# Attention with a gated layer behind it: the later head pairs' scores as 64 by 64 products, and one break per pair instead of two

## The chip, the cores and the metric

The kernel runs on one core of a Trainium2 chip. Its time is the device time of one execution in microseconds (us); the lower, the better. The data is float32 in DRAM, and the kernel starts with all inputs there.

## The reference

Causal attention of 4 batches, 12 heads, 448 positions and 64 features per head, and a gated layer of 768 to 1536 to 768 on its output:

```python
scores = (q @ k.transpose(0, 1, 3, 2)) / np.sqrt(64)      # q, k, v: (4, 12, 448, 64)
scores = np.where(np.triu(np.ones((448, 448), bool), k=1), -1e9, scores)
attn = np.exp(scores - scores.max(-1, keepdims=True))
attn = attn / (attn.sum(-1, keepdims=True) + 1e-9)
x = (attn @ v).transpose(0, 2, 1, 3).reshape(1792, 768)
gate = 1 / (1 + np.exp(-(x @ w_gate)))                    # 768 x 1536
return (gate * (x @ w_val)) @ w_out                       # w_out: 1536 x 768
```

## The kernel before

**Work.** The 48 heads are taken as 24 pairs; a pair's two heads lie in partitions 0 to 63 and 64 to 127 of the tile `raw` (448 columns of q, then 448 of k). The layers are computed batch by batch ("units" of 448 tokens): units 0 and 1 by `unit_items`, units 2 and 3 together by `pair_items`, which needs fewer products. Every layer product is split into three fast ones (`xh`,`wh`), (`xl`,`wh`), (`xh`,`wl`) of 128 x 128 by 448 columns; they stand on L610 for units 0 and 1, and on L823 for units 2 and 3. The weights of a product are loaded, and cut into `wh` (ScalarE, L591) and `wl` (VectorE or GpSimd, L593), before it; in unit 0 they come as 64-bit words (L575, 768 KB each), are put together by L579 to L583 and written back to DRAM as float32 (L586), from where the later units read them.

**Attention.** Pairs 0 to 5 are an opening of their own, ahead of the layers. Pairs 6 to 23 are called wide here. For each of them:

- `wscore` makes the scores of four blocks of queries (three of 128, the last of 64) against the keys up to the block's end: two products per block, one for each head, side by side in the two halves of the array's rows. Blocks 0 and 1 go to `s` banks, block 2 to `t` banks, block 3 to `s` banks; in block 3 the two heads' 64 queries take partitions 0 to 63 and 64 to 127.
- `wsoftmax` does the rest of the softmax: a masked minimum on VectorE (L429), exp on ScalarE (L435), sums and reciprocals on VectorE (L443, L445), the scaling on GpSimd (L450).
- `shift` transposes on VectorE (L465, L468) and sends the result through DRAM (`pd` written by L473, four loads of `pt` by L476) to finish the transposition.
- `wpv` multiplies by v (L493): 20 products of 128 rows by 64 columns of the array, each head in one half of the array's columns; its result becomes the layers' input (`features`).

**Order.** Every operation is recorded in a `Plan` with a planned cost and a due time; `Plan.order` then fixes the order on each engine by list scheduling over these, with corrections by hand in `NUDGE` (operation number to shift of the due time). TensorE runs the layers' products without end, and attention's products are put between them in breaks: `together` joins several parts into one operation that isn't cut. Before the change each wide pair n has two breaks: the scores of blocks 0 to 2; and, some 20 products later, `wpv` of pair n-2 with block 3 of pair n. `TURN` and `SPREAD` set over which stretch of the layers' products pairs 6 to 11, and 12 to 23, are spread. When the last pair's `wpv` has been recorded, `pair_inputs` makes the inputs of units 2 and 3. DMAs are issued from one queue (SP) in the planned order: an issue that waits holds up those behind it.

Of the kernel before, what the change touches and what calls it, by code (L numbers as in the profile page):

```python
# [8 lines left out]
F32 = mybir.dt.float32  # L9
# [3 lines left out]
ALU = mybir.AluOpType  # L13
# [33 lines left out]
NUDGE = {  # L47
# [4 lines left out]
}  # L52
# [151 lines left out]
def kernel(  # L204
# [21 lines left out]
    ident = new("ident", [128, 128], F32)  # L226
    mask = new("mask", [128, 4 * WQ], F32)
    pairs = [dict(b=n // HP, k=n % HP) for n in range(B * HP)]
# [166 lines left out]
    rows = lambda i: WQ if i < 3 else WL  # L395
    place = lambda z, i: slice(0, WQ) if i < 3 else slice(WL * z, WL * z + WL)
    keys = lambda i: min(WQ * (i + 1), S)

    def wscore(n, blocks, tag, due):
        j = pairs[n]  # L400
        if blocks[0] == 0:
            j["sm"] = [new("sm", [128, SMW], F32, BUFS["sm"]) for z in range(2)]
            for k in ("mn", "sum", "r"):
                j[k] = new(k, [128, 2, NB], F32, BUFS["st"])
        r = j["raw"]
        sp = [new(tag, [128, 512], F32, dict(s=3, t=2)[tag], PSUM) for z in range(2)]
        base = woff(blocks[0])
# [8 lines left out]
        burst((sum(keys(i) / 600 for i in blocks) + 0.3, mm, [(r,)], [(sp[0],), (sp[1],)]), due)  # L416
        return lambda: wsoftmax(j, blocks, sp)

    def wsoftmax(j, blocks, sp):
        base = woff(blocks[0])  # L420
        mn, su, r_ = j["mn"], j["sum"], j["r"]
        last = blocks[-1] == NB - 1
        for i in blocks:
            ne, off = keys(i), woff(i)
            o = off - base
            for z in range(2):
                y = 0 if last else z
                sm, at, s0 = j["sm"][y], place(z, i), i * WQ - place(z, i).start
                plan.op("DVE", dve(ne), lambda z=z, y=y, sm=sm, i=i, o=o, ne=ne, off=off, s0=s0, at=at: nc.vector.tensor_tensor_reduce(  # L429
                    out=sm.t[at, off:off + ne], in0=sp[z].t[at, o:o + ne], in1=mask.t[at, ZM - s0:ZM - s0 + ne],  # L430
                    scale=-0.125, scalar=3.0e38, op0=ALU.add, op1=ALU.min, accum_out=mn.t[at, y, i:i + 1],
                ), [(sp[z],), (mask,)], [(sm, (i, z)), (mn, (z, i))])
            for z in range(1 if last else 2):
                sm, zs = j["sm"][z], (0, 1) if last else (z,)
                plan.op("ACT", act(ne, 0, 1) + 0.01, lambda z=z, sm=sm, i=i, ne=ne, off=off: nc.scalar.activation(  # L435
                    out=sm.t[:, off:off + ne], in_=sm.t[:, off:off + ne], func=ACTF.Exp, scale=-1.0,
                    bias=mn.t[:, z, i:i + 1], accum_out=su.t[:, z, i:i + 1],
                ), [(mn, *[(y, i) for y in zs])], [(sm, *[(i, y) for y in zs]), (su, (z, i))], extra=0.1)
        g = (0, 0, 1, 2)[blocks[-1]]
        a = slice(blocks[0], blocks[-1] + 1)  # L440
        heads = range(1 if last else 2)
        h = slice(0, len(heads))
        plan.op("DVE", 0.13, lambda: nc.vector.tensor_scalar_add(r_.t[:, h, a], su.t[:, h, a], 1e-9),  # L443
                [(su, *[(z, i) for z in heads for i in blocks])], [(r_, g)])
        plan.op("DVE", 0.11, lambda: nc.vector.reciprocal(r_.t[:, h, a], r_.t[:, h, a]), [], [(r_, g)])  # L445
        for z in heads:
            sm = j["sm"][z]
            for i in blocks:
                o, w = woff(i), keys(i)
                plan.op("PL", 0.24 + w / 1200, lambda sm=sm, i=i, o=o, w=w, z=z: nc.gpsimd.tensor_scalar(  # L450
                    out=sm.t[:, o:o + w], in0=sm.t[:, o:o + w], scalar1=r_.t[:, z, i:i + 1], scalar2=1.0,
                    op0=ALU.mult, op1=ALU.mult), [(r_, g)], [(sm, (i, 0), (i, 1)) if last else (sm, (i, z))])

    def shift(n):
# [7 lines left out]
        for z, i in [(z, i) for i in range(3) for z in range(2)] + [(0, 3)]:  # L462
            sm, o, c, at = j["sm"][z], woff(i), min(i + 1, 3), z * 192 + ioff(i) if i < 3 else 384
            r = [(sm, (i, z))] if i < 3 else [(sm, (i, 0), (i, 1))]
# [36 lines left out]
    def burst(part, due):  # L501
        held.append(part)
# [15 lines left out]
    def att_steps(seq, wide):  # L518

        L = []  # L520
        for m in range(len(seq) + LAG + 1 if seq else 0):
# [5 lines left out]
            if wide:  # L527
                if c is not None:
                    L.append((0, lambda due, c=c: shift(c)))
                one, two = [], []  # L530
                if n is not None:
                    for bl, tag in ((0, 1), "s"), ((2,), "t"):
                        one.append((sum(keys(i) / 600 for i in bl) + 0.2, lambda due, n=n, bl=bl, tag=tag: wscore(n, bl, tag, due)))
                if d is not None:
                    two.append((2.0, lambda due, d=d: wpv(d, due)))
                if n is not None:
                    two.append((0.9, lambda due, n=n: wscore(n, (3,), "s", due)))
                for mine in (one, two):
                    if mine:
                        L.append((sum(w for w, _ in mine), lambda due, mine=mine: together(due, *(f for _, f in mine)), 1.0))  # L540
                    else:
                        L.append((0, lambda due: None, 1.0))
                continue
# [518 lines left out]
def _lay(q, k, v, moe_w_gate, moe_w_val, moe_w_out):  # L1062
# [46 lines left out]
```

## Time and profile before

| what | value |
|---|---|
| median of 3 runs (lowest, highest) | 636.79 us (636.79, 637.36) |
| the profiled execution: its time, its span | 637.35 us, 635.6 us |
| busy: TensorE, VectorE, ScalarE, GpSimd | 627.3, 455.3, 341.6, 316.0 us |
| mean granted clock of TensorE | 0.996 of full speed |
| bytes moved by DMA | 149.74 MB, 236 GB/s |

The span is what the trace covers; 1.75 us of the execution's time lie outside it. Busy time is the union of an engine's instructions, so products that run side by side count once. A float32 product that isn't split by the kernel appears as two records in the trace.

### The profile page before, as it was taken

How to read it: one execution, taken by the hardware profiler on the slowest of the kernel's cores; microseconds unless marked ns; L12 is line 12 of the kernel's file. 1: busy time of each engine (PE TensorE's matmuls, PEld its weight loads, DVE VectorE, ACT ScalarE, POOL GpSimd, SP SyncE). 2: the span in 40 equal slices, each digit the busy share in tenths (PEclk: the TensorE clock that was granted, in tenths of full speed). 3: DMA queues.
4: the chain of work that ended last, by engine and by line, in shares of the span. 5: the costliest groups of instructions: out<-in, count | busy, mean ns of one | idle time of the engine just before them, and what ended most of it. 6: DMA issues, size and time to landing. Idle time of an engine off the chain costs nothing.

```text
span 635.6 us, 10969 instructions
## 1 busy us (share of the span) xinstructions
PE 627.3 (99%) x3750; PEld 534.6 (84%) x3750; DVE 455.3 (72%) x1072; ACT 341.6 (54%) x773; POOL 316.0 (50%) x352
## 2 busy tenths in 40 slices
PE   7999999999999999999999999999999999999997
PEld 4567888888898788788787899999999989999996
DVE  4876999899975765656567965377755568999852
ACT  6877677666645555465555653442433443556520
POOL 4841524535220596676676854764765556700200
PEclk9999999999999999999999999999999999999999
DMA  7467899999998999886787884756423312444311
GB/s 276 147 229 258 308 362 387 331 365 381 308 387 339 325 333 349 303 291 245 254 309 264 289 266 155 270 213 224 156 75 124 102 49 86 134 129 143 114 74 68
DMA packets 50887, 149.74 MB, mean 236 GB/s; under 512 B 5648, under 2 KB 9104, under 8 KB 48528
## 3 DMA queue, kind: packets, MB, share of 16 engines
q1 hardware_dynamic: 50832, 149.05, 66.8%
q8 instruction: 29, 0.48, 0.3%
q14 instruction: 26, 0.21, 0.1%
HBM read 105.78 MB, written 43.25 MB: 234 GB/s over the span
## 4 chain that ended last, share of the span: by engine, by line
PE 95%; ACT 2%; POOL 1%; DVE 1%; DMA 0%; issue 0%; DVEq 0%; ACTq 0%
PE m L610 42%; PE m L823 19%; PE s L823 10%; PE t L823 7%; PE m L493 5%; PE s L414 5%; PE t L414 2%; PE s L292 2%; PE t L343 1%; POOL sm L330 1%; ACT sm L309 1%; PE m L367 1%; ACT pt L352 0%; DMA raw<-in_qkt_dram 0%; PE m L292 0%; ACT wh L591 0%
## 5 line engine op out<-in xcount | busy, mean ns | idle before, releaser
L777 POOL TENSOR_TENSOR wl<-room,wh 128x384 fp32r<-128x384 f32 x84 | 94.7, 1149 | 56.7 <-ACT wh L776 56.7
L610 PE MATMUL m<-xh,wh 128*128 128x448 f32 x288 | 109.2, 379 | 0.0
L610 PE MATMUL m<-xl,wh 128*128 128x448 f32 x288 | 105.2, 365 | 0.0
L610 PE MATMUL m<-xh,wl 128*128 128x448 f32 x288 | 105.2, 365 | 0.0
L450 POOL TENSOR_SCALAR sm<-sm,r 128x384 f32<-128x384 f32 (+3 forms) x126 | 78.9, 642 | 49.8 <-DVE r L445 39.2
L435 ACT ACTIVATE sm<-sm,mn 128x128 f32<-128x128 f32 (+3 forms) x126 | 65.8, 524 | 49.6 <-DVE mn L429 44.4
L593 POOL TENSOR_TENSOR wl<-wr,wh 128x768 fp32r<-128x768 f32 x38 | 72.7, 1916 | 35.8 <-ACT wh L591 35.2
L591 ACT CAST wh<-wr 128x768 fp32r<-128x768 f32 x72 | 59.6, 829 | 33.2 <-PE m L610 12.8
L610 PEld LDWEIGHTS m<-xh,wh 128*128 128x128 f32 x288 | 54.0, 188 | 24.2 <-issue 16.4
L776 ACT CAST wh<-room 128x384 fp32r<-128x384 f32 x84 | 39.7, 511 | 54.8 <-PE s L823 16.8
L610 PEld LDWEIGHTS m<-xh,wl 128*128 128x128 f32 x288 | 54.1, 188 | 4.4
L429 DVE CUSTOM_DVE_ANT_0 sm<-s,mask 128x128 f32<-128x128 f32 (+1 forms) x108 | 44.3, 438 | 18.4 <-PE s L414 17.5
L610 PEld LDWEIGHTS m<-xl,wh 128*128 128x128 f32 x288 | 54.2, 188 | 3.7
L610 PE MATMUL m<-gh,wh 128*128 128x448 f32 x144 | 53.4, 371 | 0.0
L610 PE MATMUL m<-gh,wl 128*128 128x448 f32 x144 | 52.6, 365 | 0.0
L610 PE MATMUL m<-gl,wh 128*128 128x448 f32 x144 | 52.6, 365 | 0.0
L640 POOL TENSOR_TENSOR gl<-gt,gh 128x448 fp32r<-128x448 f32 x24 | 29.8, 1242 | 40.4 <-ACT gh L639 21.5
L465 DVE STREAM_TRANSPOSE room<-sm 128x384 f32<-128x384 f32 (+2 forms) x84 | 34.6, 445 | 18.1 <-POOL sm L450 17.7
L823 PE MATMUL m<-pt,wh 128*128 128x448 f32 x150 | 44.8, 366 | 0.0
L593 DVE TENSOR_TENSOR wl<-wr,wh 128x768 fp32r<-128x768 f32 x34 | 35.1, 1034 | 7.8 <-ACT wh L591 7.6
L692 DVE TENSOR_TENSOR xl<-m,xh 128x448 f32<-128x448 f32 x30 | 18.6, 621 | 28.8 <-PE m L823 28.6
L493 PEld LDWEIGHTS m<-pt,vr 128*64 128x64 f32 x720 | 33.4, 137 | 5.5 <-issue 3.0
(175 smaller groups left out, 1446.9 us busy)
## 6 DMA issues: line engine op xcount, KB each, us to landing
room<-in_wp_dram SPq DMA_DIRECT2D x36, 768.0 KB, 7.7
pt<-pd SPq DMA_DIRECT2D x72, 256.0 KB, 5.1
wr<-wdram SPq DMA_DIRECT2D x45, 384.0 KB, 4.3
room<-wdram SPq DMA_DIRECT2D x45, 384.0 KB, 3.5
wdram<-wr SPq DMA_DIRECT2D x36, 384.0 KB, 7.8
pd<-room SPq DMA_DIRECT2D x12, 1024.0 KB, 5.1
raw<-in_qkt_dram SPq DMA_DIRECT2D x23, 448.0 KB, 5.5
vr<-in_vt_dram SPq DMA_DIRECT2D x24, 256.0 KB, 5.2
```

The source lines that it names most:

```text
L414: nc.tensor.matmul(out=sp[z].t[place(z, i), o:o + ne], lhsT=r.t[h, s0:s0 + rows(i)], rhs=r.t[h, S:S + ne])
L429: plan.op("DVE", dve(ne), lambda z=z, y=y, sm=sm, i=i, o=o, ne=ne, off=off, s0=s0, at=at: nc.vector.tensor_tensor_reduce(out=sm.t[at, off: ...
L435: plan.op("ACT", act(ne, 0, 1) + 0.01, lambda z=z, sm=sm, i=i, ne=ne, off=off: nc.scalar.activation(out=sm.t[:, off:off + ne], in_=sm.t[:, ...
L450: plan.op("PL", 0.24 + w / 1200, lambda sm=sm, i=i, o=o, w=w, z=z: nc.gpsimd.tensor_scalar(out=sm.t[:, o:o + w], in0=sm.t[:, o:o + w], sca ...
L465: plan.op("DVE", dve(128 * c) + 0.03, lambda sm=sm, i=i, o=o, c=c, at=at: nc.vector.transpose(out=tv()[:, :, at:at + 32 * c].rearrange("p ...
L493: nc.tensor.matmul(out=vp.t[64 * z:64 * z + 64, i * WQ:i * WQ + rows(i)], lhsT=v.t[:, c, z], rhs=src, start=(c == 0), stop=(c == i))
L591: plan.op("ACT", act(768), lambda: nc.scalar.copy(hi_.t, t.t), [(t,)], [(hi_,)])
L593: plan.op(eng, cost, lambda: at.tensor_tensor(out=lo_.t, in0=t.t, in1=hi_.t.bitcast(F32), op=ALU.subtract), [(t,), (hi_,)], [(lo_,)], lock ...
L610: nc.tensor.matmul(out=ps.t[:, :S], lhsT=a.t[:, k, :], rhs=b.t if isinstance(b, Buf) else b(), start=(first and z == 0), stop=(last and z ...
L776: plan.op("ACT", act(w), lambda: nc.scalar.copy(f(hi_.t), x()), [(src, at)], [(hi_, e)])
L777: plan.op("PL", 0.97, lambda: nc.gpsimd.tensor_tensor(out=f(lo_.t), in0=x(), in1=f(hi_.t).bitcast(F32), op=ALU.subtract), [(src, at), (hi_ ...
L823: nc.tensor.matmul(out=ps.t[:, :S], lhsT=a.t[:, kw, :], rhs=b.at, start=bool(first and z == 0), stop=bool(last and z == 2), skip_group_che ...
```

## The change

- **Products.** In all four blocks of a wide pair the scores are now products of 64 by 64 of the array (64 rows for a head's features, 64 columns for half of a block's queries): four per block, one for each quarter of the array. Block 3 has only 64 queries per head; there the four quarters are two heads by two halves of the keys (224 each). Two of these four need a head's q and k in the other half of the partitions: `_lay` appends such a copy (64 columns of q, 224 of k) to the input, and `load` brings it by a DMA of its own (128 x 288 words) into the second `sm` tile of the pair, which is not used by block 3 otherwise.
- **Banks.** Blocks 0 and 2 share the pair's two `s` banks, blocks 1 and 3 its two `t` banks; the row half of the array always writes the same bank.
- **Softmax.** Block 3 is two operations of 128 partitions x 224 columns on VectorE, the second starting from the first's minimum (`first`); before, two of 64 x 448. The mask gets 224 more columns for it (three small operations on GpSimd at the start). Sums and reciprocals are done once for blocks 0 to 2 and once for block 3.
- **Breaks.** A wide pair has one break: all its scores, then `wpv` of pair n-2.
- **Due times.** `TURN`, `SPREAD`, the start of pair 6 (0.03 to 0.0) and the table `NUDGE` are new.

```diff
-ZM = 384
+ZM = 3 * QB
+HALF = S // 2
+XW = WL + HALF
-TURN, SPREAD = 0.95, 0.85
+TURN, SPREAD = 0.97, 1.02
 NUDGE = {
-    21: 2.7, 40: -0.7, 42: 1.8, 69: -0.8, 288: 3.1, 289: 3.1, 399: 2.1, 405: 2.1, 414: 2.1, 415: 2.1, 452: 2.1,
...
+    24: 2.3, 43: -2.5, 320: 5.8, 389: 1.5, 401: 2.7, 410: 5.8, 437: -1.9, 451: -1.9, 516: 5.8, 632: 5.8,
...
     def load(n):
...
+        if n >= WIDE:
+            j["sm"] = [new("sm", [128, SMW], F32, BUFS["sm"]) for z in range(2)]
+            x = j["sm"][1]
+            plan.op("SP", dma(128 * XW * 4), lambda: nc.sync.dma_start(
+                out=x.t[:, woff(3):woff(3) + XW], in_=qkt[n][:, 2 * S:]), writes=[(x, "x")], extra=2.8)
...
+        ab = [[new(tag, [128, 512], F32, bufs, PSUM) for z in range(2)] for tag, bufs in (("s", 3), ("t", 2))]
+        sp = [ab[i % 2] for i in range(NB)]
         def mm():
-            for i in blocks:
-                s0, ne, o = i * WQ, keys(i), woff(i) - base
-                for z in range(2):
-                    h = slice(64 * z, 64 * z + 64)
-                    nc.tensor.matmul(out=sp[z].t[place(z, i), o:o + ne], lhsT=r.t[h, s0:s0 + rows(i)], rhs=r.t[h, S:S + ne])
+            for i in range(3):
+                s0, ne, o = i * WQ, keys(i), spot(i)
+                for y in range(2):
+                    for z in range(2):
+                        h, c = slice(64 * z, 64 * z + 64), 64 * (z ^ y)
+                        nc.tensor.matmul(out=sp[i][z].t[c:c + 64, o:o + ne],
+                                         lhsT=r.t[h, s0 + c:s0 + c + 64], rhs=r.t[h, S:S + ne])
+            for y in range(2):
+                for z in range(2):
+                    h, c = slice(64 * z, 64 * z + 64), z ^ y
+                    q, k = (x.t[h, woff(3):woff(3) + WL], x.t[h, woff(3) + WL:woff(3) + XW]) if y else (
+                        r.t[h, 3 * WQ:S], r.t[h, S + HALF * z:S + HALF * (z + 1)])
+                    o = spot(3)
+                    nc.tensor.matmul(out=sp[3][z].t[64 * c:64 * c + 64, o:o + HALF], lhsT=q, rhs=k)
...
-                one, two = [], []
+                mine = []
                 if n is not None:
-                    for bl, tag in ((0, 1), "s"), ((2,), "t"):
-                        one.append((sum(keys(i) / 600 for i in bl) + 0.2, lambda due, n=n, bl=bl, tag=tag: wscore(n, bl, tag, due)))
+                    mine.append((2.0, lambda due, n=n: wscore(n, due)))
                 if d is not None:
-                    two.append((2.0, lambda due, d=d: wpv(d, due)))
-                if n is not None:
-                    two.append((0.9, lambda due, n=n: wscore(n, (3,), "s", due)))
+                    mine.append((2.0, lambda due, d=d: wpv(d, due)))
```

How the program's order changes, at three places (equal rows that follow each other are one row with a count; the last words are the output's shape).

TensorE, one pair in the middle of the kernel, before: its two breaks, `wscore` on L414 and `wpv` on L493, with L610's products between them left out.

```order
L414 MATMUL s<-raw 128x128 x2
L414 MATMUL s<-raw 128x256 x2
L414 MATMUL t<-raw 128x384 x2
...
L493 MATMUL m<-pt,vr 64x128 x12
L493 MATMUL m<-pt,vr 64x64 x8
L414 MATMUL s<-raw 64x448 x2
```

The same on TensorE now, where `wscore` stands on L427 and L435, `wpv` on L515 and the layers' products of units 0 and 1 on L628.

```order
L427 MATMUL s<-raw 64x128 x4
L427 MATMUL t<-raw 64x256 x4
L427 MATMUL s<-raw 64x384 x4
L435 MATMUL t<-raw 64x224 x2
L435 MATMUL t<-sm 64x224 x2
L515 MATMUL m<-pt,vr 64x128 x12
L515 MATMUL m<-pt,vr 64x64 x8
```

Eight products of a pair's scores have become 16, and nothing of L628 stands between them and `wpv` any more. In the middle 36 to 72 products of L628 stand between two breaks; before it were 18 to 24 for most. By the 648 products of unit 0 the scores of 8 wide pairs and `wpv` of 6 are done, before and now, in 17 breaks before and 10 now.

SP, the queue that issues the DMAs, in the middle of the kernel, now (L495 writes a pair's `pd`, L498 loads its `pt`, L279 is the new load, L606 brings weights).

```order
L495 DMA pd<-room 128x2048
L279 DMA sm<-in_qkt_dram 128x288
L606 DMA wr<-wdram_1774 128x768
L606 DMA wr<-wdram_1811 128x768
L285 DMA vr<-in_vt_dram 128x512
L273 DMA raw<-in_qkt_dram 128x896
L498 DMA pt<-pd 128x512 x4
```

The new load of pair n+2 stands right behind the write of pair n's `pd`, as it does in all but the first and last pairs; both wait for pair n's transposes.

TensorE, where units 0 and 1 end and units 2 and 3 begin, now (L841 is the layers' product there, before on L823).

```order
L628 MATMUL m<-gh_4240,wl 128x448
L841 MATMUL t<-xh_4159,wh 128x448
L841 MATMUL t<-xl_4171,wh 128x448
L841 MATMUL t<-xh_4159,wl 128x448
L515 MATMUL m<-pt,vr 64x128 x12
L515 MATMUL m<-pt,vr 64x64 x8
L841 MATMUL t<-xh_4164,wh 128x448
```

The last pair's `wpv` has moved from 108 products ahead of units 2 and 3 to 3 products behind their start. Between the last pair's scores and its `wpv` stand `wpv` of two pairs and 111 products now; before, from its block 3 on, one `wpv` and 90 products.

## Rows read from the trace of the kernel before

**Rows 1.** The page: busy time by engine, then the chain's shares by engine.

```profile
PE 627.3 (99%) x3750; PEld 534.6 (84%) x3750; DVE 455.3 (72%) x1072; ACT 341.6 (54%) x773; POOL 316.0 (50%) x352
...
PE 95%; ACT 2%; POOL 1%; DVE 1%; DMA 0%; issue 0%; DVEq 0%; ACTq 0%
```

**Rows 2.** Waits of TensorE, first and last of four: us in total, times, longest.

```profile
PE s L292 <- DMA raw<-in_qkt_dram: 3.4, 1, 3.4
...
PE s L292 <- DVE mn L305: 0.3, 1, 0.3
```

**Rows 3.** The chain in order of time: start us, us, engine, tile, line, records.

```profile
254.79 0.86 PE s L414 x8
256.29 4.45 PE m L610 x21
260.74 1.93 PE m L493 x40
262.67 0.90 PE s L414 x4
263.56 4.46 PE m L610 x21
...
348.29 5.07 PE m L610 x24
...
355.28 0.90 PE s L414 x4
...
366.81 9.92 PE m L610 x48
376.73 1.93 PE m L493 x40
378.66 22.08 PE m L610 x108
```

**Rows 4.** Timeline of TensorE's weight loads: start, us, operation, shapes, count [idle before].

```profile
247.43 1.86 PEld L493 LDWEIGHTS m<-pt,vr 128*64 128x64 f32 x40 [0.30 <-ACT wh L591]
```

**Rows 5.** Windows: PE, PEld, DVE, ACT, POOL busy us (count); PEclk; DMA share; GB/s.

```profile
70.00:130.00 60.00, 60.00 (x364) 50.62 (x363) 56.90 (x139) 39.68 (x84) 31.44 (x36) 1.00 0.97 353
...
170.00:180.00 10.00, 10.00 (x62) 9.05 (x62) 8.34 (x23) 4.34 (x9) 5.91 (x7) 1.00 0.94 324
180.00:190.00 10.00, 10.00 (x74) 9.29 (x69) 5.95 (x9) 4.82 (x7) 0.00 (x0) 1.00 1.02 419
190.00:200.00 10.00, 10.00 (x54) 9.02 (x54) 4.76 (x6) 3.50 (x5) 0.00 (x0) 1.00 1.03 407
```

**Rows 6.** Timeline of VectorE and TensorE near 207 us: a weight's second half, and its first use.

```profile
206.32 1.16 DVE L593 TENSOR_TENSOR wl<-wr,wh 128x768 fp32r<-128x768 f32 x1 [0.42 <-ACT wh L591]
...
208.18 0.36 PE L610 MATMUL m<-gh,wl 128*128 128x448 f32 x1
```

**Rows 7.** Timeline of the queue SP (the last pair's DMAs); the page's landing time of `pt`.

```profile
362.66 0.32 SPq L473 DMA_DIRECT2D pd<-room  x1
...
368.30 1.74 SPq L476 DMA_DIRECT2D pt<-pd  x4
...
pt<-pd SPq DMA_DIRECT2D x72, 256.0 KB, 5.1
```

**Rows 8.** Timeline of TensorE before the first wide pair; the page's landing time of `raw`.

```profile
50.38 0.74 PE L343 MATMUL t<-ident,sm 112*112 112x112 f32 x4
...
58.38 0.93 PE L414 MATMUL s<-raw 64*128 64x128 f32 x8
...
raw<-in_qkt_dram SPq DMA_DIRECT2D x23, 448.0 KB, 5.5
```

**Rows 9.** Timeline of VectorE in block 3, and of GpSimd near the start.

```profile
208.33 0.60 DVE L429 CUSTOM_DVE_ANT_0 sm<-s,mask 64x448 f32<-64x448 f32 x1
208.87 0.07 DVE L429 DVE_READ_ACCUMULATOR2_ANT mn<- 64x1 f32 x1
...
10.57 1.92 POOL L330 TENSOR_SCALAR sm<-sm,r 112x112 f32<-112x112 f32 x4 [8.12 <-ACT sm L309]
```

More of the change, by code (lines that the diff above doesn't have):

```diff
@@ L226 @@
     ident = new("ident", [128, 128], F32)
-    mask = new("mask", [128, 4 * WQ], F32)
+    mask = new("mask", [128, ZM + WQ + HALF], F32)
     pairs = [dict(b=n // HP, k=n % HP) for n in range(B * HP)]
@@ L249, in keep @@
             plan.op("PL", 0.6, lambda: nc.gpsimd.affine_select(
-                out=t.t, in_=t.t, pattern=[[-1, n]], compare_op=cmp, fill=v, base=base, channel_multiplier=1
+                out=t.t[:, :n], in_=t.t[:, :n], pattern=[[-1, n]], compare_op=cmp, fill=v, base=base, channel_multiplier=1
             ), writes=[(t,)])
         fill(mask, 0.0)
-        keep(mask, 4 * WQ, ALU.is_ge, -8.0e9, ZM)
+        keep(mask, ZM + WQ, ALU.is_ge, -8.0e9, ZM)
         fill(ident, 1.0)
         keep(ident, 128, ALU.is_equal, 0.0, 0)
+        end = lambda: mask.t[:, ZM + WQ + HALF - WL:]
+        for step, base, v in (-1, -WL, -8.0e9), (0, -WL, 0.0), (-1, 0, -8.0e9):
+            plan.op("PL", 0.3, lambda step=step, base=base, v=v: nc.gpsimd.affine_select(
+                out=end(), in_=end(), pattern=[[step, WL]], compare_op=ALU.is_ge, fill=v, base=base, channel_multiplier=1
+            ), [(mask,)], [(mask, "end")])
     def load(n):
@@ L395, with wscore @@
     rows = lambda i: WQ if i < 3 else WL
-    place = lambda z, i: slice(0, WQ) if i < 3 else slice(WL * z, WL * z + WL)
     keys = lambda i: min(WQ * (i + 1), S)
-    def wscore(n, blocks, tag, due):
+    spot = lambda i: (384, 0, 0, 256)[i]
+    def wscore(n, due):
         j = pairs[n]
[L401 to L407, printed above, removed]
-        def mm():
+        for k in ("mn", "sum", "r"):
+            j[k] = new(k, [128, 2, NB], F32, BUFS["st"])
+        r, x = j["raw"], j["sm"][1]
+        ab = [[new(tag, [128, 512], F32, bufs, PSUM) for z in range(2)] for tag, bufs in (("s", 3), ("t", 2))]
+        sp = [ab[i % 2] for i in range(NB)]
+        def mm():
+            for i in range(3):
[12 more added lines that the diff above has]
+                    nc.tensor.matmul(out=sp[3][z].t[64 * c:64 * c + 64, o:o + HALF], lhsT=q, rhs=k)
+        burst((1.95, mm, [(r, 0, 1), (x, "x")], [(p,) for p in ab[0] + ab[1]]), due)
+        return lambda: wsoftmax(j, sp)
@@ L410, in mm, with wsoftmax @@
+    def wsoftmax(j, sp):
+        mn, su, r_ = j["mn"], j["sum"], j["r"]
+        for blocks in (0, 1, 2), (3,):
+            last = blocks[0] == 3
+            heads = range(1 if last else 2)
             for i in blocks:
-                s0, ne, o = i * WQ, keys(i), woff(i) - base
+                ne, off, o = keys(i), woff(i), spot(i)
                 for z in range(2):
-                    h = slice(64 * z, 64 * z + 64)
-                    nc.tensor.matmul(out=sp[z].t[place(z, i), o:o + ne], lhsT=r.t[h, s0:s0 + rows(i)], rhs=r.t[h, S:S + ne])
@@ L416, in wscore @@
[L416 to L422, printed above, removed]
-        for i in blocks:
-            ne, off = keys(i), woff(i)
-            o = off - base
-            for z in range(2):
[L427 to L452, printed above, removed]
@@ new lines, in wsoftmax @@
+                    sm, n = j["sm"][0 if last else z], HALF if last else ne
+                    f, lo = (off + HALF * z, (ZM + WQ) * z) if last else (off, ZM - i * WQ)
+                    to = 1 - z if last else z
+                    first = lambda z=z, i=i, last=last: mn.t[:, 1, i:i + 1] if last and z else 3.0e38
+                    plan.op("DVE", dve(n), lambda z=z, i=i, sm=sm, n=n, o=o, f=f, lo=lo, to=to, first=first: nc.vector.tensor_tensor_reduce(
+                        out=sm.t[:, f:f + n], in0=sp[i][z].t[:, o:o + n], in1=mask.t[:, lo:lo + n], scale=-0.125, scalar=first(),
+                        op0=ALU.add, op1=ALU.min, accum_out=mn.t[:, to, i:i + 1],
+                    ), [(sp[i][z],), (mask, "end") if last and z else (mask,)] + ([(mn, (1, i))] if last and z else []),
+                        [(sm, (i, z) if last else i), (mn, (to, i))])
@@ new lines, in wsoftmax @@
+                for z in heads:
+                    sm = j["sm"][z]
+                    plan.op("ACT", act(ne, 0, 1) + 0.01, lambda z=z, sm=sm, i=i, ne=ne, off=off: nc.scalar.activation(
+                        out=sm.t[:, off:off + ne], in_=sm.t[:, off:off + ne], func=ACTF.Exp, scale=-1.0,
+                        bias=mn.t[:, z, i:i + 1], accum_out=su.t[:, z, i:i + 1],
+                    ), [(mn, (z, i))], [*([(sm, (i, 0), (i, 1))] if last else []), (sm, i), (su, (z, i))], extra=0.1)
+            a = slice(blocks[0], blocks[-1] + 1)
@@ new lines, in wsoftmax @@
+            h = slice(0, len(heads))
+            plan.op("DVE", 0.13, lambda h=h, a=a: nc.vector.tensor_scalar_add(r_.t[:, h, a], su.t[:, h, a], 1e-9),
+                    [(su, *[(z, i) for z in heads for i in blocks])], [(r_, last)])
+            plan.op("DVE", 0.11, lambda h=h, a=a: nc.vector.reciprocal(r_.t[:, h, a], r_.t[:, h, a]), [], [(r_, last)])
+            for z in heads:
+                sm = j["sm"][z]
+                for i in blocks:
+                    o, w = woff(i), keys(i)
+                    plan.op("PL", 0.24 + w / 1200, lambda sm=sm, i=i, o=o, w=w, z=z: nc.gpsimd.tensor_scalar(
+                        out=sm.t[:, o:o + w], in0=sm.t[:, o:o + w], scalar1=r_.t[:, z, i:i + 1], scalar2=1.0,
+                        op0=ALU.mult, op1=ALU.mult), [(r_, last)], [(sm, i)])
@@ L463, in shift @@
             sm, o, c, at = j["sm"][z], woff(i), min(i + 1, 3), z * 192 + ioff(i) if i < 3 else 384
[L464 removed]
+            r = [(sm, i)]
             plan.op("DVE", dve(128 * c) + 0.03, lambda sm=sm, i=i, o=o, c=c, at=at: nc.vector.transpose(
@@ L470, in shift @@
             in_=sm.t[:, woff(3) + 384:woff(3) + 448].rearrange("p (r j) -> p r j", j=32)),
-            [(j["sm"][0], (3, 0), (3, 1))], [(tb, "end")])
+            [(j["sm"][0], 3)], [(tb, "end")])
         pd = new("pd", [128, 4 * WC], F32, 2, bass.MemoryType.DRAM)
@@ L529, in att_steps @@
                     L.append((0, lambda due, c=c: shift(c)))
-                one, two = [], []
+                mine = []
                 if n is not None:
-                    for bl, tag in ((0, 1), "s"), ((2,), "t"):
-                        one.append((sum(keys(i) / 600 for i in bl) + 0.2, lambda due, n=n, bl=bl, tag=tag: wscore(n, bl, tag, due)))
+                    mine.append((2.0, lambda due, n=n: wscore(n, due)))
                 if d is not None:
-                    two.append((2.0, lambda due, d=d: wpv(d, due)))
-                if n is not None:
-                    two.append((0.9, lambda due, n=n: wscore(n, (3,), "s", due)))
[L538 to L542, printed above, removed]
+                    mine.append((2.0, lambda due, d=d: wpv(d, due)))
+                if mine:
+                    L.append((sum(w for w, _ in mine), lambda due, mine=mine: together(due, *(f for _, f in mine)), 1.0))
+                else:
+                    L.append((0, lambda due: None, 1.0))
                 continue
@@ L1027 @@
     att = []
-    for seq, wide, lo, hi in ((range(HP, WIDE), False, 0.0, 0.03), (range(WIDE, 2 * HP), True, 0.03, TURN), (last, True, TURN, 1 + SPREAD)):
+    for seq, wide, lo, hi in ((range(HP, WIDE), False, 0.0, 0.03), (range(WIDE, 2 * HP), True, 0.0, TURN), (last, True, TURN, 1 + SPREAD)):
         steps = att_steps(seq, wide)
@@ L1067, in _lay @@
     qkt[0] = np.concatenate([x[:, :2 * QB], x[:, S:], x[:, 2 * QB:S]], axis=1)
+    qkt = np.concatenate([qkt, np.zeros((B * HP, 128, XW), qkt.dtype)], axis=2)
+    x = qkt[WIDE:]
+    for z, (lo, hi) in enumerate(((0, HALF), (HALF, S))):
+        a, b = slice(64 * z, 64 * z + 64), slice(64 - 64 * z, 128 - 64 * z)
+        x[:, a, 2 * S:2 * S + WL] = x[:, b, 3 * WQ:S]
+        x[:, a, 2 * S + WL:] = x[:, b, S + lo:S + hi]
     vt = np.zeros((B * HP, 128, NB, 2, D), v.dtype)
```

7 rows, old and new, of the table NUDGE are left out of this document.

## The prediction, made before the changed kernel ran

> **What bounds the kernel now.** I read the page first, then TensorE's waits, the chain in order of time, and the windows. TensorE is busy for 627.3 us of the 635.6 us span and makes up 95% of the chain [rows 1]. It waits for another engine or a DMA four times in all, 3.4 us for the first load and 0.3 to 0.6 us for the rest, all in the opening [rows 2]. From 57 us on, the chain is TensorE's own work in its own order [rows 3]. So each us that leaves TensorE's stream leaves the time, as long as what it consumes (weights, `pt`) comes earlier by as much.
>
> The price of a break is read from the chain's pieces [rows 3]. 108 products of L610 take 22.08 us and 48 take 9.92 us: (22.08 - 9.92) / 60 = 0.203 us for a product, and 9.92 - 48 x 0.203 = 0.19 us left over for a run between two breaks, whatever its length (21 products: 4.45 - 4.26 = 0.19). A break thus costs 0.19 us beside its own work. One wide pair in the steady part:
>
> - blocks 0 to 2, from 254.79 to 256.29: 1.50 us
> - `wpv`: 1.93 us
> - block 3, from 262.67 to 263.56: 0.90 us
> - two breaks: 0.38 us, together 4.71 us.
>
> **The change, part by part.** *Block 3.* Two products of 448 columns, side by side on two of the array's four quarters, become four of 224 columns on all four. If four quarters run at once, the columns that pass halve, and so does the time: 0.90 to 0.45 us. Rows 3 show each pairing but never four at once. Block 3 gives 0.90 / 448 = 2.0 ns per column of a product. Blocks 0 to 2 have 6 products with 1536 columns, 3.1 us at that price one after the other; they take 1.50 us, so the two row halves run side by side. `wpv` has 20 products with 2048 columns, 4.1 us one after the other; it takes 1.93, so the two column halves do too, though both use all the rows.
>
> *Blocks 0 to 2.* Twelve products of 64 by 64 replace six of 64 by 128. With four at once, the columns that pass are the same 768: 1.50 us again. Bounds: not below, since no column goes. Above: with two at a time, twice as much, 3.0 us (a rival, below). In between: if a block's second pair of products starts only as the first pair's second record does, the last record of block 3 stands alone, 0.22 us (half of its new 0.45 us). The number of instructions is not the limit by `wpv`, which puts 40 records and 40 weight loads through in 1.93 us, 48 ns each; the new scores have 32 in 1.95 us. I take 1.50.
>
> A rule of the Trainium skill speaks against this. What the trace shows: in `wpv` the two column halves use the same rows, and its 40 weight loads keep the loader busy for 1.86 us [rows 4] of the 1.93 us [rows 3] in which products run on without a wait. The Trainium skill, TensorE: Matmul & The Clock Gate, section Part 3: Packing small matmuls, says that a weight load overlaps a running matmul only if the two use different row groups. By that rule the two quarters of one row half would take turns, and the sum would be the first rival's 660 us; `wpv` by the same rule would take some 4.1 us, and the trace does not agree.
>
> *Breaks.* 18 score breaks and 20 others (18 with block 3, two with `wpv` alone) become 20. Sum of TensorE over the 18 wide pairs: before 18 x (1.50 + 1.93 + 0.90) + 38 x 0.19 = 85.2 us; now 18 x (1.50 + 1.93 + 0.45) + 20 x 0.19 = 73.6 us. Gain 11.5 us; 7.5 us with the lone 0.22 us for each pair.
>
> *VectorE, GpSimd, DMA.* Block 3 on VectorE falls from two operations of 0.54 us (208.33 to 208.87) [rows 9] to two of half the columns, some 0.5 us less a pair, and one pair of small sums and reciprocals goes. That is off the chain, but it helps at 70 to 130 us, where VectorE is busy for 56.9 us of 60 [rows 5]. The three mask operations fall into GpSimd's idle 8.12 us before 10.57 us [rows 9]: nothing. The new load is 147 KB a pair. For the first wide pair it can start when the transposes of pair 4 end (51.1 us) and, by the landing time of the larger `raw`, 5.5 us, is there at 56.6 us, ahead of the scores at 58.4 us [rows 8]: nothing, but with 2 us to spare.
>
> **What is late next.** Two covers get thin.
>
> First, the weights of unit 0. From 180 to 200 us the DMA engines are full (share 1.02 and 1.03 at 419 and 407 GB/s) [rows 5], and at the end of that a weight's second half is ready at 207.48 us and used at 208.18 [rows 6]: 0.7 us of slack. By the end of unit 0, 8 pairs have saved 0.45 us each and 7 breaks are gone: TensorE comes 8 x 0.45 + 7 x 0.19 = 4.9 us earlier. If the transfers don't come earlier too, 4.9 - 0.7 = 4.2 us are given back there, for good. The eight new loads by then (1.2 MB, 2.9 us at 407 GB/s) work in the same direction. Against it: at 170 to 180 us the DMA moved 324 GB/s, so there is room ahead of the full stretch. Between 0 and 4.2 us I take 2.5 us.
>
> Second, `pt`. The last pair's six first blocks end at 348.29 us and its block 3 at 356.18 [rows 3]; its `pd` is issued at 362.66, the last of its `pt` by 370.04, and lands some 4.7 us later (5.1 us from issue), near 374.7 [rows 7]; `wpv` starts at 376.73. From the end of block 3 to landing it is 18.5 us, from the end of the six blocks 26.4 us. Now all scores end together, and `wpv` follows two breaks later: in the middle, with 42 and 48 products between, 1.93 + (42 x 0.203 + 0.19) + 3.88 + (48 x 0.203 + 0.19) + 1.95 = 26.4 us; for the last pair 2 x 1.93 + 111 x 0.203 + 3 x 0.19 = 27.0 us. So the spare time is between 0 and 8 us. I take 0.5 us for all pairs together; 1 us a pair would be 12 us. Behind a waiting `wpv` nothing on TensorE can pass.
>
> Sum: 637.35 - 11.5 + 2.5 + 0.5 = 628.85 us for an execution like the profiled one, which is 0.56 us above the median of 636.79: 628.3 us.
>
> **The rivals.**
>
> *Quarters take turns* (slower). If only two of four run at once, a pair's scores cost 1.50 + 0.45 = 1.95 us more than I count, 35 us over 18 pairs: 636.8 - 11.5 + 35.1 = 660 us. It decides from 0.64 us more a pair (11.5 / 18). For it: no row has four at once. Against it: both pairings run freely [rows 3, 4], and the four need nothing that these two don't.
>
> *The gain waits* (no change, or slightly slower). Full DMA engines give back 4.2 us, `pt` comes 0.3 to 0.7 us late for each of the last 12 pairs (4 to 8 us), or the last `wpv`, now 3 products into units 2 and 3, holds those up: 633 to 638 us. For it: 0.7 us of slack and the lower end of `pt`'s spare time. Against it: TensorE never waits after the opening now, and VectorE has less to do.
>
> *Four at once, but not freely* (a smaller gain): the lone 0.22 us for each pair and full give-back, 7.5 - 4.2 - 0.5 = 2.8 us: 634 us; without give-back 629 us.
>
> *Nothing is given back* (counted as the low end of the forecast): 636.8 - 11.5 = 625 us.
>
> **How the numbers follow.** My forecast with 0 to 4.2 us of give-back (624 to 630 us, the low end with 1 us for what the new due times may do to the opening) 0.60; four not freely (629 to 634) 0.13; the gain waits 0.14; quarters take turns 0.13. The time of the likeliest is 628.3 us. The range reaches from 624 to 637.5 us and leaves out the turns, most of all. No change is within 0.2% (1.3 us, about what a measurement tells from none): a third of "the gain waits", 0.05; slower is the turns and a sixth of it, 0.15; the rest, 0.80, is faster.
>
> **What would show it.** Right: in the chain the pieces of L427 and L435 together take 1.9 to 2.0 us, L515 1.93 us, with one leftover of 0.19 us; four records of a block start within some ns of each other; TensorE's waits after 57 us are few, near 200 to 230 us, for `wl` or the weights' DMA. Wrong: pieces of L427 of 3 us (turns); waits of L515 for `pt` pair after pair; a wait of L841 for the weights or inputs of units 2 and 3 right behind the last L515; or an opening that ends later than 58 us.

## The result, and the profile after

The changed kernel takes 625.67 us (median of 4 runs, 625.09 to 627.05) against 636.83 us for the kernel before in the same measurement (636.79 to 637.36): a ratio of 0.9826, 95% interval 0.9808 to 0.9844. That is 11.2 us less. Forecast were 628.3 us, 8.5 us less, in a range from 624 to 637.5 us. The profiled execution took 625.28 us, its span is 623.6 us (before 637.35 and 635.6).

Busy time by engine, and the chain's shares by engine, from the page of the changed kernel; they answer to [rows 1].

```profile
PE 612.9 (98%) x4038; PEld 532.6 (85%) x4038; DVE 448.9 (72%) x1036; ACT 339.0 (54%) x773; POOL 310.9 (50%) x355
...
PE 87%; ACT 4%; DVE 3%; DMA 2%; POOL 2%; issue 2%; SPq 0%; DVEq 0%; POOLq 0%; ACTq 0%
```

TensorE is busy for 14.4 us less, though it has 288 records more. It is still nearly always busy, but its share of the chain fell from 95% to 87%: for some stretches something else now ends last.

The chain in order of time of the changed kernel, one pair in the middle; it answers to [rows 3].

```profile
243.73 0.38 PE s L427 x8
244.11 0.43 PE t L427 x8
244.54 0.64 PE s L427 x8
245.19 0.38 PE t L435 x8
245.56 1.93 PE m L515 x40
247.49 9.92 PE m L628 x48
```

All scores of a pair take 0.38 + 0.43 + 0.64 + 0.38 = 1.83 us, from 243.73 to 245.56, where before blocks 0 to 2 took 1.50 and block 3 0.90, together 2.40. `wpv` takes the same 1.93 us. The run of 48 products takes the same 9.92 us as before, so 0.19 us are left over for a break, as before.

The timeline of TensorE in one pair's scores, changed kernel.

```profile
231.19 0.45 PE L427 MATMUL s<-raw 64*64 64x128 f32 x8
231.46 0.61 PE L427 MATMUL t<-raw 64*64 64x256 f32 x8
231.89 0.82 PE L427 MATMUL s<-raw 64*64 64x384 f32 x8
232.54 0.36 PE L435 MATMUL t<-raw 64*64 64x224 f32 x2
232.55 0.36 PE L435 MATMUL t<-sm 64*64 64x224 f32 x2
232.73 0.36 PE L435 MATMUL t<-raw 64*64 64x224 f32 x2
232.74 0.35 PE L435 MATMUL t<-sm 64*64 64x224 f32 x2
233.02 2.00 PE L515 MATMUL m<-pt,vr 128*64 128x128 f32 x40
```

Here the four quarters are seen at once: block 3's first four records (two from `raw`, two from the copy in `sm`) start at 232.54 and 232.55, their second four 0.19 us later.

TensorE's waits after the opening, from the list of waits of the changed kernel (us in total, times, longest); before there were none.

```profile
PE m L628 <- DVE wl L611: 0.3, 1, 0.3
...
PE m L841 <- DVE xl L710: 0.3, 1, 0.3
```

The timeline of TensorE and VectorE at the first of these; it answers to [rows 6].

```profile
183.87 0.36 PE L628 MATMUL m<-gl,wh 128*128 128x448 f32 x1
184.55 0.47 PE L628 MATMUL m<-gh,wl 128*128 128x448 f32 x1 [0.32 <-DVE wl L611]
...
183.54 0.96 DVE L611 TENSOR_TENSOR wl<-wr,wh 128x768 fp32r<-128x768 f32 x1 [0.96 <-ACT wh L609]
```

From 183.87 to 184.55 it is 0.68 us between two products instead of 0.20: 0.48 us lost for a weight that is ready at 184.50. Another 0.27 us are lost at 219.38, and 0.25 us more than before near 521 us. Together that is 1.0 us of give-back; with the wider steps next to these three (0.28 to 0.31 us instead of 0.20) it is 1.4 us.

Windows of the changed kernel; they answer to [rows 5].

```profile
160.00:170.00 10.00, 10.00 (x51) 9.27 (x50) 8.38 (x17) 5.70 (x10) 6.19 (x9) 1.00 1.01 384
170.00:180.00 10.00, 10.00 (x80) 9.09 (x79) 7.52 (x12) 5.17 (x7) 0.00 (x0) 1.00 0.98 356
180.00:190.00 10.00, 9.68 (x46) 8.31 (x46) 5.36 (x7) 3.71 (x5) 0.00 (x0) 1.00 1.02 405
```

The DMA engines are full from 160 us on now, where before 170 to 180 us ran at 0.94 and 324 GB/s: the transfers have moved ahead with TensorE.

The whole account, from the starts of TensorE's records between the first wide pair's scores and the end: scores 43.2 us before, 33.0 us now, 10.2 less; `wpv` 34.65 and 34.66 us; products of units 0 and 1 with their breaks and waits 264.4 and 261.9 us, 2.5 less, of which 0.6 are three products that now run earlier, in the opening; units 2 and 3 0.3 us more to the start of their last product.

The 1.9 us that remain in units 0 and 1 are a difference. These products stand in 39 runs before and 21 now; at 0.19 us each, 18 runs fewer are 3.4 us less. So some 1.5 us are given back there: 1.15 us at the two waits near 184 and 219 us, and 0.6 us in two runs (81 products from 92.47 us, 72 from 343.20) that start a product every 0.207 us instead of every 0.203, with no wait in the list; the kernel before loses 0.2 us in such runs. What slows them is not shown.

The two profiled executions differ by 12.1 us, the medians by 11.2. The one of the kernel before has a stretch at the lower clock in its opening:

```profile
12.99:16.40 3.41, 3.41 (x20) 2.49 (x18) 2.05 (x6) 2.59 (x6) 2.94 (x6) 0.50 0.39 143
```

Its first wide pair starts at 58.38 us; in before_pv_less_early (below), the same program up to there without such a stretch, it starts at 57.79. So some 0.6 us of the 12.1 are no gain. The changed kernel starts its first wide pair at 58.52 us with three products of L628 (0.6 us) more done: the opening itself takes about as long as before.

### The profile page after: what moved, and what is told of

It reads as the page before. It is cut to its first block, busy times and chain, and to the rows that moved or that the text cites. A ratio compares the mean times of both kernels' runs of the same rounds, so it can differ in the third digit from the quotient of the medians.

```text
span 623.6 us, 11552 instructions
## 1 busy us (share of the span) xinstructions
PE 612.9 (98%) x4038; PEld 532.6 (85%) x4038; DVE 448.9 (72%) x1036; ACT 339.0 (54%) x773; POOL 310.9 (50%) x355
## 4 chain that ended last, share of the span: by engine, by line
PE 87%; ACT 4%; DVE 3%; DMA 2%; POOL 2%; issue 2%; SPq 0%; DVEq 0%; POOLq 0%; ACTq 0%
PE m L628 37%; PE m L841 19%; PE s L841 10%; PE t L841 7%; PE m L515 5%; PE s L427 3%; ACT sm L323 2%; DMA wdram<-wr 1%; PE t L427 1%; PE s L306 1%; PE t L435 1%; PE t L357 1%; POOL sm L472 1%; PE m L381 1%; POOL sm L344 1%
## 5 line engine op out<-in xcount | busy, mean ns | idle before, releaser
L795 POOL TENSOR_TENSOR wl<-room,wh 128x384 fp32r<-128x384 f32 x84 | 98.8, 1199 | 56.5 <-ACT wh L794 52.3
L628 PE MATMUL m<-xh,wh 128*128 128x448 f32 x288 | 107.5, 373 | 0.0
L472 POOL TENSOR_SCALAR sm<-sm,r 128x256 f32<-128x256 f32 (+3 forms) x126 | 70.3, 578 | 74.0 <-DVE r L467 40.4
L628 PE MATMUL m<-xh,wl 128*128 128x448 f32 x288 | 105.4, 366 | 0.1
L628 PE MATMUL m<-xl,wh 128*128 128x448 f32 x288 | 105.3, 365 | 0.0
L611 POOL TENSOR_TENSOR wl<-wr,wh 128x768 fp32r<-128x768 f32 x38 | 69.9, 1857 | 18.7 <-ACT wh L609 18.5
L459 ACT ACTIVATE sm<-sm,mn 128x256 f32<-128x256 f32 (+3 forms) x126 | 65.5, 523 | 7.3 <-DVE mn L452 7.3
L628 PEld LDWEIGHTS m<-xh,wh 128*128 128x128 f32 x288 | 54.1, 188 | 7.0 <-issue 1.8
L628 PEld LDWEIGHTS m<-xh,wl 128*128 128x128 f32 x288 | 54.1, 188 | 4.8 <-POOL wl L611 0.5
L628 PEld LDWEIGHTS m<-xl,wh 128*128 128x128 f32 x288 | 54.2, 188 | 4.0
L628 PE MATMUL m<-gh,wh 128*128 128x448 f32 x144 | 53.6, 372 | 0.0
L628 PE MATMUL m<-gh,wl 128*128 128x448 f32 x144 | 52.8, 367 | 0.3 <-DVE wl L611 0.3
L628 PE MATMUL m<-gl,wh 128*128 128x448 f32 x144 | 52.7, 366 | 0.0
L841 PE MATMUL m<-pt,wh 128*128 128x448 f32 x150 | 44.8, 367 | 0.3 <-DVE xl L710 0.3
L452 DVE CUSTOM_DVE_ANT_0 sm<-s,mask 128x128 f32<-128x128 f32 (+1 forms) x72 | 29.3, 417 | 19.7 <-PE s L427 19.7
L611 DVE TENSOR_TENSOR wl<-wr,wh 128x768 fp32r<-128x768 f32 x34 | 34.7, 1019 | 11.2 <-ACT wh L609 10.9
L515 PEld LDWEIGHTS m<-pt,vr 128*64 128x64 f32 x720 | 33.4, 137 | 5.9 <-issue 4.9
L601 DVE SCALAR_TENSOR_TENSOR wr<-room,wr 128x768 int32<-128x768 int32 x36 | 36.7, 1020 | 0.5
```

Source lines behind the costliest of these rows:

```text
L515: nc.tensor.matmul(out=vp.t[64 * z:64 * z + 64, i * WQ:i * WQ + rows(i)], lhsT=v.t[:, c, z], rhs=src, start=(c == 0), stop=(c == i))
L601: plan.op("DVE", 0.87, lambda: nc.vector.scalar_tensor_tensor(out=ri(), in0=lo(), scalar=29, in1=ri(), op0=ALU.logical_shift_right, op1=AL ...
L611: plan.op(eng, cost, lambda: at.tensor_tensor(out=lo_.t, in0=t.t, in1=hi_.t.bitcast(F32), op=ALU.subtract), [(t,), (hi_,)], [(lo_,)], lock ...
L628: nc.tensor.matmul(out=ps.t[:, :S], lhsT=a.t[:, k, :], rhs=b.t if isinstance(b, Buf) else b(), start=(first and z == 0), stop=(last and z ...
L795: plan.op("PL", 0.97, lambda: nc.gpsimd.tensor_tensor(out=f(lo_.t), in0=x(), in1=f(hi_.t).bitcast(F32), op=ALU.subtract), [(src, at), (hi_ ...
L841: nc.tensor.matmul(out=ps.t[:, :S], lhsT=a.t[:, kw, :], rhs=b.at, start=bool(first and z == 0), stop=bool(last and z == 2), skip_group_che ...
```

## The experiments

My theory: the gain is TensorE's own time, first from the four quarters in block 3, then from fewer breaks; a little is given back in waits. The rivals: the merged break and the new due times bring it, whatever form the products have; or the gain was larger and went back through the new load or the supply of weights.

**block3_alone: the four quarters of block 3 put into the kernel before.** Everything else of the products is as before (two breaks, the old due times, 64 by 128 in blocks 0 to 2); the new load and the longer mask come with it. The planned cost of block 3 is lower too, and the order is another one between 178 and 221 us.

```diff
     def mm():
+        if blocks[0] == 3:
+            for y in range(2):
+                for z in range(2):
...
+                    nc.tensor.matmul(out=sp[z].t[64 * c:64 * c + 64, :HALF], lhsT=q, rhs=k)
+            return
         for i in blocks:
```

Expected:

> The kernel before, with block 3 alone in four quarters (its two breaks, its due times and its 64 by 128 products in blocks 0 to 2 kept; the new load and the longer mask added). If four quarters at once are where the gain comes from, block 3's piece falls from 0.90 to about 0.48 us: 18 x 0.42 = 7.6 us less, 629 us (627.5 to 631). If the gain came from the merged break and the new due times, about 637 us, as before. If the extra load in the same queue costs something in unit 0, up to 3 us above 629.

Measured: 631.98 us (631.76 to 632.05), ratio to before 0.9920 (0.9907 to 0.9934): 4.8 us less, not 7.6. The chain in order of time of this kernel:

```profile
251.95 0.86 PE s L437 x8
252.81 0.65 PE t L437 x4
253.45 4.45 PE m L640 x21
257.90 1.93 PE m L523 x40
259.83 0.54 PE s L431 x8
```

Block 3 fell from 0.90 to 0.54 us, 18 x 0.36 = 6.5 us. Some 1.4 us of that are lost between 204 and 221 us, where the order has shifted: 0.5 us in steps that end with a weight (at 204.49 and 209.22), and 0.87 us at one pair, whose blocks 0 to 2 now follow block 3 of the pair ahead at once and wait until VectorE has read scores (L452):

```profile
218.59 0.49 PE L437 MATMUL s<-raw 64*128 64x128 f32 x2
219.47 0.70 PE L437 MATMUL s<-raw 64*128 64x128 f32 x5 [0.40 <-DVE mn L452]
```

The rival that it is the breaks and due times alone falls: with no break merged and no due time changed, over two fifths of the gain are there. My number missed by 0.06 us a pair, 1.1 us in all, and by the 1.4 us of these waits, which I had not counted.

**wide_rows: blocks 0 to 2 as 64 by 128 again,** in the changed kernel; only block 3 is in quarters.

```diff
-                for y in range(2):
-                    for z in range(2):
-                        h, c = slice(64 * z, 64 * z + 64), 64 * (z ^ y)
-                        nc.tensor.matmul(out=sp[i][z].t[c:c + 64, o:o + ne],
-                                         lhsT=r.t[h, s0 + c:s0 + c + 64], rhs=r.t[h, S:S + ne])
+                for z in range(2):
+                    h = slice(64 * z, 64 * z + 64)
+                    nc.tensor.matmul(out=sp[i][z].t[:, o:o + ne], lhsT=r.t[h, s0:s0 + WQ], rhs=r.t[h, S:S + ne])
```

Expected:

> The changed kernel, with blocks 0 to 2 as six products of 64 by 128 again, block 3 in quarters, one break. If only the columns that pass count, 625.7 us, within 0.6. If a change between the two ways of dividing the array costs what one costs elsewhere (0.1 to 0.15 us between wpv and block 3 before), and the first weights of 128 columns cost 0.05 us more, 18 x 0.15 to 0.20 = 2.7 to 3.6 us more: 628.8 us. If 64 by 64 products had been costly in themselves, less than 625 us.

Measured: 629.59 us (629.40 to 630.32), ratio to before 0.9885 (0.9872 to 0.9899), 3.9 us above the changed kernel. The timeline of TensorE in one pair's scores:

```profile
246.19 0.49 PE L426 MATMUL s<-raw 64*128 64x128 f32 x4
246.51 0.60 PE L426 MATMUL t<-raw 64*128 64x256 f32 x4
246.95 0.81 PE L426 MATMUL s<-raw 64*128 64x384 f32 x4
247.69 0.41 PE L433 MATMUL t<-raw 64*64 64x224 f32 x2
...
248.23 0.98 PE L513 MATMUL m<-pt,vr 128*64 128x128 f32 x14
```

From 246.19 to 248.23 it is 2.04 us, 0.21 more than the 1.83 of the changed kernel, and 18 x 0.21 = 3.8 us. Against the timeline above, start to start: block 0 takes 0.32 us instead of 0.27; block 1, 0.44 and 0.43; block 2, at whose end the array changes its division, 0.74 instead of 0.65; block 3, 0.54 instead of 0.48. So the form 64 by 64 saves nothing in columns, as counted, but it keeps all scores in one division of the array. Block 3 takes 0.54 us wherever it follows another division, here and in block3_alone.

The Trainium skill, TensorEngine Tiling (Array Packing), section Key Properties, says that changing the tiling mode, not just the tile, drains TensorE. The trace agrees as far as it goes: block 1, with no change of division at either end, differs by 0.01 us, and block 2, with one at its end, by 0.09 us. The page gives no figure for it.

**two_breaks: `wpv` in a break of its own,** a few products behind the scores, in the changed kernel.

```diff
+APART = 2.5
...
+    def apart(due, *steps):
...
+        for e, p in enumerate(parts):
+            plan.op("PE", p[0], p[1], p[2], p[3], due + APART * e, count=e == 0)
...
-                    L.append((sum(w for w, _ in mine), lambda due, mine=mine: together(due, *(f for _, f in mine)), 1.0))
+                    L.append((sum(w for w, _ in mine), lambda due, mine=mine: apart(due, *(f for _, f in mine)), 1.0))
```

(`count` keeps the added operations out of the numbers that `NUDGE` uses.) Expected:

> The changed kernel, with wpv put behind up to 12 more of the layers' products, in a break of its own, in 15 of the 16 pairs where it stood behind the scores. If a break costs by itself (0.15 to 0.19 us), 2.3 to 2.9 us more than the changed kernel: 628.3 us. If the merging is not where time went, 625.7 us, within 0.5.

Measured: 629.07 us (628.06 to 630.90), ratio to before 0.9878 (0.9861 to 0.9895), 3.4 us above the changed kernel. From the list of waits of this kernel, then its chain in order of time at one pair's `wpv`:

```profile
PE m L520 <- DMA vr<-in_vt_dram: 1.1, 1, 1.1
...
PE m L520 <- ACT gt L664: 0.9, 1, 0.9
...
PE m L520 <- DMA pt<-pd: 0.2, 1, 0.2
```

```profile
261.08 0.80 PE m L643 x3
261.89 1.93 PE m L520 x40
263.81 9.32 PE m L643 x45
```

The trace has 14 pairs whose `wpv` follows scores at once in the changed kernel, not 16, and 13 of them are apart here: 35 breaks instead of 22, of which one was in units 2 and 3. A run of three products takes 0.80 us, 0.19 more than three times 0.203, and one of 45 leaves 0.19 over too: the price of a break is 0.19 us, as read before the change, even for a run this short. The products of units 0 and 1 with their breaks and waits take 4.2 us more in the profiled execution (266.1 us for 261.9), of which 14 breaks are 2.7 us. The rest is waits: 2.2 us of `wpv` are new, and 0.8 us that the changed kernel lost near 184 us are gone. These come from the other order.

**no_copy: without the new load.** Block 3's second pair of products takes q and k of the wrong head from `raw`, so the output isn't the reference's.

```diff
-            plan.op("SP", dma(128 * XW * 4), lambda: nc.sync.dma_start(
-                out=x.t[:, woff(3):woff(3) + XW], in_=qkt[n][:, 2 * S:]), writes=[(x, "x")], extra=2.8)
...
-                    q, k = (x.t[h, woff(3):woff(3) + WL], x.t[h, woff(3) + WL:woff(3) + XW]) if y else (
-                        r.t[h, 3 * WQ:S], r.t[h, S + HALF * z:S + HALF * (z + 1)])
+                    q, k = r.t[h, 3 * WQ:S], r.t[h, S + HALF * z:S + HALF * (z + 1)]
```

Expected:

> The changed kernel without the new load: block 3's second pair of products takes q and k of the wrong head from raw, so its result isn't the reference's. If the load is hidden, at most the two waits for weights near 184 and 219 us (0.75 us in all) go: 625 to 625.7 us. If the full DMA engines of unit 0 pay for the loads, 2 to 3 us less: 623 us.

Measured: 625.64 us (625.14 to 625.97), ratio to before 0.9823 (0.9810 to 0.9837): the changed kernel's time. In its profiled execution the two waits near 184 and 219 us are gone, and a wait of 0.3 us of `wpv` for its `vr` near 190 us is there instead. So the new load costs nothing that stands out from the spread of these runs.

**pv_less_early and before_pv_less_early: how much room the supply of TensorE has in unit 0.** For pairs 6 to 11, `wpv` does 8 of its 20 products (each block of queries takes its own 128 keys alone, so the output isn't the reference's), in the changed kernel and in the kernel before. The planned order is the same.

```diff
-                for c in range(i + 1):
+                for c in range(i if b < PAIR else 0, i + 1):
...
-                                         start=(c == 0), stop=(c == i))
+                                         start=(c == (i if b < PAIR else 0)), stop=(c == i))
```

Expected of the first:

> The changed kernel with 8 of the 20 products of wpv for pairs 6 to 11 (each block of queries takes its own 128 keys alone, so the result isn't the reference's); the planned order is unchanged. wpv falls from 1.93 to some 0.9 us. If TensorE still sets the time at 90 to 190 us, 6 x 1.05 = 6.3 us less than the changed kernel: 619.4 us. If the supply of unit 0's weights sets it now (slack of 0.5 us from 163 us on), nearly nothing less: 624 to 625.7 us.

and of the second:

> The kernel before with the same 12 products of wpv left out for pairs 6 to 11. If the supply of weights had room of about 5 us there, the room that the change has used, nearly all of 6.3 us: 630.5 to 632 us. If it had none but the 0.7 us of slack near 208 us, 635.5 to 636.5 us.

Measured: 622.78 us (622.67 to 623.02), 2.9 us less than the changed kernel; and 631.94 us (631.69 to 632.76), 4.9 us less than the kernel before (ratios to before 0.9779, 0.9764 to 0.9793, and 0.9924, 0.9909 to 0.9939). In both, `wpv` takes 6.0 us less on TensorE (34.65 to 28.62 us). So the kernel before kept 4.9 of 6.0 us, and the changed kernel 2.9 of 6.0. Windows of pv_less_early, then its two longest waits behind the opening:

```profile
160.00:170.00 10.00, 8.63 (x55) 7.61 (x54) 9.10 (x19) 4.34 (x8) 5.79 (x9) 1.00 1.00 375
...
180.00:190.00 10.00, 9.39 (x56) 7.69 (x55) 5.57 (x8) 4.67 (x7) 0.00 (x0) 1.00 1.04 415
```

```profile
PE m L515 <- DMA vr<-in_vt_dram: 1.4, 1, 1.4
...
PE s L427 <- DMA raw<-in_qkt_dram: 0.6, 1, 0.6
```

TensorE is idle for 1.37 us in the first of these windows and 0.61 us in the second, with the DMA engines full. The first is the wait for a pair's v, the second two waits for weights: what runs short is what the DMAs bring as a whole, weights and a pair's own loads, and not the weights alone. Both of my cases were too plain: TensorE could come 4.9 us earlier before the change, and can come 2.9 us earlier still after it, though its 648th product of L628 starts at 210.26 us now against 216.55 before (L610), 0.6 of which is the lower clock in the opening.

**pv_less_late: the same for pairs 12 to 23,** in the changed kernel (`b >= PAIR` in the lines above; again not the reference's output). Expected:

> The changed kernel with the same 12 products of wpv left out for pairs 12 to 23 instead. If TensorE sets the time in units 1 to 3, 12 x 1.05 = 12.6 us less than the changed kernel: 613 us. If pt or the weights are about to take over there, waits of L515 or L628 give back a part: 616 us or more.

Measured: 618.78 us (617.59 to 619.88), ratio to before 0.9715 (0.9700 to 0.9730): 6.9 us less than the changed kernel of the 12.1 us that `wpv` saves (34.66 to 22.59 us). Waits of this kernel, then TensorE's timeline at the longest:

```profile
PE m L628 <- POOL wl L611: 1.8, 1, 1.8
```

```profile
346.44 0.37 PE L628 MATMUL m<-gl,wh 128*128 128x448 f32 x1
348.64 0.48 PE L628 MATMUL m<-gh,wl 128*128 128x448 f32 x1 [1.84 <-POOL wl L611]
```

Here GpSimd sets the time: it cuts the weights (L611) and scales the scores (L472), and a weight comes 2.0 us late. The stretch at the lower clock behind it (last section) costs 1.5 us more, so 3.5 of the 5.2 us that don't arrive are lost at this one place. So TensorE is the bound in unit 1 only by a narrow margin too. Units 2 and 3 begin 6.0 us earlier (380.15 us for 386.14) and take as long as in the changed kernel, 235.5 us without the last `wpv`: there nothing is given back.

**no_nudge: the changed kernel with an empty `NUDGE`.**

```diff
-NUDGE = {
-    24: 2.3, 43: -2.5, 320: 5.8, 389: 1.5, 401: 2.7, 410: 5.8, 437: -1.9, 451: -1.9, 516: 5.8, 632: 5.8,
...
-}
+NUDGE = {}
```

Expected:

> The changed kernel with an empty table NUDGE. If the new table carries part of the gain by taking waits away, several us more than the changed kernel (628 to 634 us), with waits of TensorE in the trace that show where. If it doesn't matter, 625.7 us, within 1.

Measured: 629.31 us (628.51 to 630.43), ratio to before 0.9886 (0.9870 to 0.9903), 3.6 us above the changed kernel. From its list of waits:

```profile
PE m L622 <- DVE wl L605: 1.1, 3, 0.5
...
PE m L622 <- ACT wh L603: 0.3, 1, 0.3
```

Between 160 and 200 us its products lose 3.1 us in steps of 0.4 to 0.7 us, all for weights, where the changed kernel loses 0.9 us in the same runs of products. So two thirds of the gain need no table, and the table's part is to keep the weights ahead of TensorE in unit 0. The kernel before has a table of its own; what it would take without one no run shows.

## Why the prediction was right

The mechanism was right but for one cost that it left out, that of a change between two divisions of the array. Four sizes were off, and that the time came within 2.6 us of the forecast is partly luck, since the misses have both signs.

- **Block 3 in four quarters: 0.45 us less a pair forecast.** In kind as forecast: all four quarters run at once, and the rival in which they take turns (660 us) is out, by the starts at 232.54 and 232.55. Taken by itself it is 0.36 us (block3_alone), 1.6 us less over 18 pairs than forecast. Block 3 takes 0.54 us behind another division and 0.48 us behind its own, so the change of division is a part that doesn't halve.
- **Blocks 0 to 2 at no change: mis-sized, the largest miss.** I counted columns, which stayed. The form 64 by 64 saves 0.21 us a pair by keeping one division through all scores (wide_rows, 3.9 us in all). Together 0.57 us a pair instead of 0.45, 1.83 us where 1.9 to 2.0 were forecast: 10.2 us of scores instead of 8.1.
- **Breaks: 18 fewer, 3.4 us forecast.** The price of 0.19 us holds, by the runs of 48 products in the changed kernel and of 3 in two_breaks. The count was off: the traces have 39 breaks before, not 38, as `wpv` stands alone three times and not two, and 22 now, not 20, as it stands alone four times. The 17 fewer are 3.2 us.
- **Give-back: 3.0 us forecast, some 1.7 us measured** (1.5 us in units 0 and 1, and 0.2 us near 521 us). I took 2.5 of at most 4.2 us for unit 0's weights, as 0.7 us was the smallest slack near 208 us and the DMA engines were full from 180 to 200 us. The slack near 208 us was that of one weight in an order that the change rearranges; before_pv_less_early shows that the supply of the kernel before could follow a TensorE that is 6 us faster for all but 1.1 us. Part of the room was where I had named it and not counted it: at 170 to 180 us the DMA engines still had some.
- **Together** 10.2 + 3.2 - 1.7 = 11.7 us less, against 11.2 us between the medians.
- **`pt`: 0.5 us forecast.** No wait of L515 is in the trace of the changed kernel. For its last pair the scores end at 360.2 us, the last `pt` load is issued at 380.3 and `wpv` starts at 386.91; with 4.7 us to landing that is 2 us of spare time, inside the bounds of 0 to 8 us.
- **The rule on weight loads.** The Trainium skill's TensorE: Matmul & The Clock Gate, Part 3: Packing small matmuls, lets a load overlap a running product only in another row group; the four records within 0.02 us share two row groups, two each, and start together behind block 2, which runs on the same rows; the trace does not agree, as it didn't in `wpv`.

What stays open: how much of the 11.2 us comes from `TURN` and `SPREAD`. They were not tried alone, since the numbers in `NUDGE` belong to one order of recording.

## What to carry to other kernels

Where small products fill half an array, cutting them so that every part of the array works halves their columns; count the changes of division too, and put products of one division next to each other, even at more instructions. A wait-free bound engine says nothing about how far its suppliers can follow: take a little work off it in the trace's narrowest stretch and see how much of it the time keeps. Slack read at one place belongs to one order, and an order that is made anew moves it.

## What the runs showed of the hardware that I had not expected

In pv_less_late TensorE waited 1.84 us at 346.80 and ran on at 348.64 with products every 0.20 us; then its granted clock fell. Windows of that kernel:

```profile
346.00:349.00 3.00, 1.16 (x6) 0.74 (x6) 2.55 (x7) 1.30 (x2) 3.00 (x6) 1.00 0.76 290
349.00:350.30 1.30, 1.30 (x7) 1.20 (x6) 1.30 (x3) 0.00 (x0) 1.30 (x1) 0.89 0.65 88
350.30:353.10 2.80, 2.80 (x9) 2.48 (x8) 2.35 (x1) 0.00 (x0) 1.87 (x2) 0.50 1.00 396
353.10:356.00 2.90, 2.90 (x45) 1.71 (x45) 0.66 (x5) 1.26 (x2) 0.90 (x1) 0.95 0.97 373
```

From 350.3 to 353.1 us the clock is 0.50, the lower of its two levels (1.2 GHz), although TensorE was busy again from 348.64 on, and nine products take 0.37 us each: some 1.5 us more on top of the 2.0 us of the wait. So this wait cost nearly twice what the list of waits shows. That the wait brought the lower clock about is read from their order alone; the 1.37 us in which TensorE was idle in pv_less_early were not followed by one.
